# One of seven output products split once more into seven, over two couples of row tiles

## Chip, cores and metric

The kernel runs on one core of a Trainium2 chip. The metric is the device time of one execution in microseconds. Three runs of the kernel before gave a median of 860.69 us (860.5 to 860.8).

## The reference

`x` is [2048, 640]. The kernel computes attention over the last 512 cached keys of 32 heads of width 192, projects the result back to 640 columns, and gates it with a feed-forward block:

```python
xn = _layernorm(x)
q  = (xn @ wq)                                   # 32 heads of 192
p  = softmax(q @ k[-512:].T * 192 ** -0.5)
s  = concat_heads(p @ v[-512:]) @ wo             # [2048, 6144] @ [6144, 640]
g  = _silu((silu(xn @ w_gate) * (xn @ w_up)) @ w_down)
return x + s * g
```

The change concerns only `s`, that is the product with `wo`, and how it is computed for 12 of the 16 row tiles.

## The kernel before, in words

First the layer norm and the feed-forward block are computed; `g` goes to a DRAM buffer, `g_d`. Then come 32 phases of attention, whose order is written out by hand in tables of tokens. The attention output is transposed by DMA and written to DRAM, `o_d`, as 16 row tiles of 128 rows with 48 chunks of the contraction of 128 each. The output part multiplies it with `wo`.

In the output part, a **couple** is a pair of row tiles (`ROW_PAIRS`, eight couples, numbered 0 to 7). For a couple the product is a 2 x 2 block product: the left matrix has quarters A11, A12 (first row tile, the two halves of the contraction) and A21, A22 (second row tile); `wo` has quarters B11 to B22, split by contraction half and column half. A quarter on the left is 24 chunks of 128 x 128; on the right 24 chunks of 128 x 320. The eight block products are replaced by seven (M1 to M7, in the order M1, M7, M2, M5, M6, M4, M3) with sums of quarters on both sides (`A_OF`, `B_OF`). `product` (L1201) issues one of them: 24 matmuls of 320 columns into one PSUM bank, each with its own weight load. M2 accumulates in the bank of M1, M4 in that of M7, M3 in that of M5.

- The left sums (`a_sum`, L1193, VectorE, 128 x 3072) take M7 = A11 - A21, M5 = A21 + A22, M6 = M5 - A11, M3 = A12 - M6. They go in turn to two places in `q_all` and to one tile `a_s`, three sums ahead of the product that uses them.
- The right sums (`b_sum`, L1165) are made once, during the end of attention and the first two couples.
- ScalarE copies the banks of M1 and M7 to SBUF (`u` and `v`). VectorE adds the products up there (`total`, L1238) and applies the gate and `x` (`finish`, L1222 and L1223, two operations for a quarter of the output).
- The left quarters lie in four tiles `a_q` for couples of even number and four for odd. `load_a` (L1178, 768 KB) brings couple n+2 into the tiles of couple n: A11 and A21 are issued after M6 of couple n, A12 and A22 after its M4. `load_xg` and `store` bring `x` and `g` in and the result out. All of these stand in order in SyncE's queue (SP).
- Products of couples 0 and 1 alternate; couples 2 to 7 run one after another (`ORDER`).
- In the very last couple, M5 and M3 go as two halves of 160 columns each into two banks, so that the first half can be finished earlier.

Eight PSUM banks serve the output part (`bank`, pool `psum_out`), handed out by the framework as earlier tiles are no longer used.

Of the kernel before, what the change touches and what calls it, by code (L numbers as in the profile page):

```python
# [10 lines left out]
ALU = mybir.AluOpType  # L11
# [4 lines left out]
def kernel(  # L16
# [13 lines left out]
    nc = tc.nc  # L30
    P = nc.NUM_PARTITIONS
# [8 lines left out]
    W = min(4096, max(256, Sk // 4))  # L40
# [10 lines left out]
    KH = NPAIR * PD // P // 2  # L51
    HC = D // 2
# [4 lines left out]
    h16 = dt.float16  # L57
# [23 lines left out]
    def mm_tile(which=None):  # L81
# [11 lines left out]
    q_all = qpool.tile([P, 16, 512], bf, name="q_all")  # L93
# [5 lines left out]
    A11, A12, A21, A22 = range(4)  # L99
    M1, M7, M2, M5, M6, M4, M3 = PRODUCTS = range(10, 17)  # L100
    A_OF = {
        M1: (A11,), M2: (A12,), M4: (A22,),
        M7: (A11, A21, ALU.subtract), M5: (A21, A22, ALU.add), M6: (M5, A11, ALU.subtract),
        M3: (A12, M6, ALU.subtract),
    }
# [152 lines left out]
    a_q, b_w = {}, {}  # L258
# [882 lines left out]
    def load_b(m, pool=None, eng=nc.scalar, c0=0, c1=KH):  # L1141
        if m in b_w:
            pass
        elif pool is None:
            b_w[m] = xc[:, 0:3, :, :].rearrange("p s c n -> p (s c n)").rearrange("p (c d) -> p c d", d=HC)
        else:
            b_w[m] = b_tile(m, pool)[:, :, :]
        if eng is None:
            return
        to = b_w[m][:, c0:c1, :]  # L1150
        eng.dma_start(out=to.bitcast(bf) if m in B_SUMS else to, in_=wo_quarter(m, c0, c1))
# [28 lines left out]
    late, a_s, xg = [], {}, {}  # L1180

    def a_sum(n, m):
        x, y, op = A_OF[m]
        k = len(a_s) % 3
        if k == 2:
            a_s[n, m] = late[0].tile([P, KH, P], h16, name="a_s", tag="a_s")
        else:
            a_s[n, m] = q_all[:, 8 * k : 8 * k + 6, :].bitcast(h16).rearrange("p a (c n) -> p (a c) n", n=P)

        def part(q):  # L1190
            return a_s[n, q] if q in A_OF and (n, q) in a_s and len(A_OF[q]) == 3 else a_q[n, q][:]

        nc.vector.tensor_tensor(a_s[n, m][:] if k == 2 else a_s[n, m], part(x), part(y), op)  # L1193
# [12 lines left out]
    def load_xg(n):  # L1206
        for side, r in enumerate(ROW_PAIRS[n]):
            tag, bufs = ("khat", 2) if n % 2 == 0 else (("K_p", "KT")[side], 1)
            t = xg[n, side] = kpool.tile([P, 2, D], bf, name="xg", tag=tag, bufs=bufs)
            nc.sync.dma_start(out=t[:, 0, :], in_=x2[r * P : (r + 1) * P, :])  # L1210
            nc.sync.dma_start(out=t[:, 1, :], in_=g_d[r, :, :])
# [17 lines left out]
    V = nc.vector  # L1229

    ORDER = [(n, m) for ms in ((M1, M7), (M2,), (M5,), (M6,), (M4,), (M3,)) for n in range(2) for m in ms][1:]
    ORDER += [(n, m) for n in range(2, len(ROW_PAIRS)) for m in PRODUCTS]
    A_SUMS = [nm for nm in ORDER if len(A_OF[nm[1]]) == 3]

    acc = {}
# [4 lines left out]
    def bank(n, name):  # L1240
        acc[n, name] = late[1].tile([P, 512], f32, name="acc")[:, 0:HC]
        return acc[n, name]
# [16 lines left out]
    def run(n, m):  # L1259

        ahead = n + 2 < len(ROW_PAIRS)
        u, v, c = (f_tile(n, k) for k in range(3))
        if m == M1:
            ps = bank(n, "M1+M2")
            product(n, M1, ps)
            nc.scalar.copy(u, ps)  # L1266
        elif m == M7:
            ps = bank(n, "M7+M4")
            product(n, M7, ps)
            nc.scalar.copy(v, ps)  # L1270
        elif m == M2:
            ps = acc[n, "M1+M2"] if n else bank(n, "M2")
            product(n, M2, ps, first=n == 0)
            if n == 0:
                total(f_tile(n, 3), ps, u)
            finish(n, 0, 0, ps if n else f_tile(n, 3), in_psum=n > 0)
            if (n, M3) == ORDER[-1]:
                store(n, 0, slice(0, HC))
        elif m == M5:
            pss = [bank(n, "M5+M3"), bank(n, "M5+M3'")] if (n, M3) == ORDER[-1] else [bank(n, "M5+M3")]  # L1280
            product(n, M5, pss)
            w = HC // len(pss)
            for k, ps in enumerate(pss):
                total(v[:, k * w : (k + 1) * w], ps[:, 0:w], v[:, k * w : (k + 1) * w])
        elif m == M6:
            ps = bank(n, "M6")
            product(n, M6, ps)
            total(u, ps, u)
            total(v, u, v)
            finish(n, 1, 1, v)  # L1290
            for q in (A11, A21) if ahead else ():
                load_a(n + 2, q)
        elif m == M4:
            ps = acc[n, "M7+M4"]
            product(n, M4, ps, first=False)
            total(c, ps, u)
            finish(n, 1, 0, c)
            for q in (A12, A22) if ahead else ():
                load_a(n + 2, q)
            store(n, 1)  # L1300
        else:
            ps, t, last_cols = acc[n, "M5+M3"], xg[n, 0], slice(HC, D)
            if (n, m) == ORDER[-1]:
                total(u, u, t[:, 1, last_cols], ALU.mult)
                total(u, u, t[:, 0, last_cols])
                pss = [ps, acc[n, "M5+M3'"]]
                product(n, M3, pss, first=False)
                w = HC // len(pss)
                for k, ps in enumerate(pss):
                    part, cols = slice(k * w, (k + 1) * w), slice(HC + k * w, HC + (k + 1) * w)  # L1310
                    total(c[:, part], ps[:, 0:w], t[:, 1, cols], ALU.mult)
                    total(t[:, 0, cols], c[:, part], u[:, part])
                    store(n, 0, cols, (nc.sync, nc.scalar)[k])
            else:
                product(n, M3, ps, first=False)
                total(u, ps, u)
                finish(n, 0, 1, u)
                store(n, 0)
            if ahead:
                load_xg(n + 2)  # L1320
        if (n, m) in A_SUMS:
            k = A_SUMS.index((n, m)) + 3
            if 3 < k < len(A_SUMS):
                a_sum(*A_SUMS[k])

    FIRST = (
# [40 lines left out]

    AHEAD = task_tables()
    groups, units = {}, {}
    wide = None  # L1370

    def group_of(s, kind):

# [28 lines left out]
             "wc": combine_wq, "wp": lambda pr: combine_wq(pr, 2), "j": join_wq}[what[:-1]](pr, *n)  # L1402

    def token(s, x):
        nonlocal wide

        cp, ph = divmod(s, 4)
        if x[0].isdigit():
            context_unit(s, *x.split("."))
        elif x[0] == "s" and x[1].isdigit():  # L1410
            scores(first_step(s) + int(x[1]) // KC, int(x[1]) % KC)
        elif x[:2] == "sp":
            spill(first_step(s) + int(x[2]))
        elif x[:2] in ("DG", "JG"):
            q_diag(JOINT if x[0] == "J" else 1 if ph < 2 else 0, *x[2:])
        elif x[0] in "RJ":
            group_of(s, x[0])[x[1]](*x[2:])
        elif x[:2] in ("TT", "QQ"):
            k, j = (int(x[2]), 2) if x[0] == "T" else divmod(int(x[2]), 2)
            q_rows(first_step(s + 1) + k, j, int(x[3]))  # L1420
        elif x == "ah":
            if s in AHEAD:
                what, *args = AHEAD[s]
                what(*args)
        elif x[:2] == "vl":
            pr = 2 * cp + (1 if x[2] == "O" else 2 if s else 0)
            if pr < NPAIR:
                load_v(pr)
        elif x == "free":
            actx.close()  # L1430
            wide = ctx.enter_context(tc.tile_pool(name="out_b", bufs=1, reuse_waits="tile"))
            O_last = wide.tile([P, 2, 4, 2, Dh], bf, name="O_last")
            O_late.extend(O_last[:, k, :, :, :] for k in range(2))
        elif x[:3] == "lM5":
            n = int(x[3])
            load_b(M5, None, nc.sync, n * KH // 4, (n + 1) * KH // 4)
        elif x[0] == "l":
            load_a("AB".index(x[1]), int(x[2]))
        elif x[:2] == "xg":
            load_xg(int(x[2]))  # L1440
        elif x[:2] == "bm":
            b_sum(M7, int(x[2]))
        elif x[0] == "o":
            first_product(int(x[1]))
        elif x == "as0":
            a_sum(*A_SUMS[0])
        else:
            what, n = (x[:-1], (int(x[-1]),)) if x[-1].isdigit() else (x, ())
            of_pair(s, what, n)
# [26 lines left out]
    for k, (n, m) in enumerate(ORDER):  # L1476
        run(n, m)
        for step in sums.get((n, m), ()):
            b_sum(*step)
        if (n, m) == (1, M1):  # L1480
            a_sum(*A_SUMS[3])
        if k < 4:
            load_b(M3, late[0], nc.sync, k * KH // 4, (k + 1) * KH // 4)


# [28 lines left out]
```

## Time and profile before

| | |
|---|---|
| median of three runs | 860.69 us (860.5 to 860.8) |
| the profiled execution, its time | 860.93 us |
| its span in the profile | 859.0 us |
| TensorE busy, in the span | 854.2 us, 99% |
| VectorE busy | 601.7 us, 70% |
| ScalarE busy | 456.4 us, 53% |
| granted TensorE clock | 1.0 |
| output part: couples 2 to 7 begin with M1 at | 718.56 us |
| last product begins at | 852.28 us |

The span runs from the first to the last instruction of the profiled execution; what lies around it is the difference to its time. PE is TensorE's matmuls, PEld its weight loads, DVE VectorE, ACT ScalarE, SP SyncE's DMA queue. A matmul's own duration overlaps that of the next, so what one costs is seen from the distance between starts.

### The profile page before, as it was taken

How to read it: one execution, taken by the hardware profiler on the slowest of the kernel's cores; microseconds unless marked ns; L12 is line 12 of the kernel's file. 1: busy time of each engine (PE TensorE's matmuls, PEld its weight loads, DVE VectorE, ACT ScalarE, POOL GpSimd, SP SyncE). 2: the span in 40 equal slices, each digit the busy share in tenths (PEclk: the TensorE clock that was granted, in tenths of full speed). 3: DMA queues.
4: the chain of work that ended last, by engine and by line, in shares of the span. 5: the costliest groups of instructions: out<-in, count | busy, mean ns of one | idle time of the engine just before them, and what ended most of it. 6: DMA issues, size and time to landing. Idle time of an engine off the chain costs nothing.

```text
span 859.0 us, 23271 instructions
## 1 busy us (share of the span) xinstructions
PE 854.2 (99%) x9839; PEld 571.5 (67%) x9839; DVE 601.7 (70%) x1059; ACT 456.4 (53%) x611; POOL 165.6 (19%) x247
## 2 busy tenths in 40 slices
PE   9999999999999999999999999999999999999998
PEld 6456446577667667667667667667677777777776
DVE  6687987877758758757757767767657796555564
ACT  4574675657667666676676676676766500000000
POOL 0010000103324324324323323323412000000000
PEclk9999999999999999999999999999999999999999
DMA  9879314556787799998999996899699998745400
GB/s 294 180 139 214 77 35 108 133 94 157 179 176 127 184 206 178 192 216 176 200 210 191 198 174 147 185 186 197 161 158 195 284 294 293 253 153 188 168 27 16
DMA packets 271496, 149.14 MB, mean 174 GB/s; under 512 B 174112, under 2 KB 267296, under 8 KB 271392
## 3 DMA queue, kind: packets, MB, share of 16 engines
q1 hardware_dynamic: 270608, 147.01, 75.3%
q8 instruction: 77, 1.26, 0.7%
q10 hardware_dynamic: 784, 0.65, 0.3%
q14 instruction: 27, 0.22, 0.1%
HBM read 80.51 MB, written 30.41 MB: 129 GB/s over the span
## 4 chain that ended last, share of the span: by engine, by line
PE 99%; DMA 1%; SPq 0%; DVE 0%; issue 0%
PE acc L1201 21%; PE sc L1047 19%; PE mm L1085 13%; PE mm L990 13%; PE sc L990 7%; PE sc L1085 6%; PE sc L394 6%; PE mm L479 3%; PE mm L637 3%; PE sc L637 2%; PE sc L479 2%; PE mm L978 1%; PE sc L690 1%; DMA wg_sb<-in_B_w_gate_dram 1%; PE gu L394 0%; PE mm L1251 0%
## 5 line engine op out<-in xcount | busy, mean ns | idle before, releaser
L1051 ACT ACTIVATE p_t<-sc 128x1024 bf16<-128x1024 f32 x256 | 256.9, 1025 | 93.9 <-PE sc L1047 93.2
L1047 PE MATMUL sc<-q_all,khat 64*128 64x512 bf16 x1536 | 204.5, 376 | 0.0
L1085 PEld LDWEIGHTS <-p_t 64*128 64x128 bf16 x4096 | 180.2, 94 | 35.2 <-POOL turn_t L1063 0.3
L1085 PE MATMUL mm<-V_p,p_t 64*128 64x193 bf16 x2784 | 146.9, 243 | 0.0
L990 PEld LDWEIGHTS <-w_all 64*128 64x128 f16 (+1 forms) x1540 | 87.3, 94 | 72.8
L990 PE MATMUL mm<-xc,w_all 64*128 64x512 f16 x950 | 119.4, 376 | 0.0
L1047 PEld LDWEIGHTS <-khat 64*128 64x128 bf16 x1536 | 83.2, 94 | 50.8 <-issue 2.4
L1032 POOL TENSOR_TENSOR m_f<-m_f 128x1024 f32<-128x1024 f32 x44 | 104.8, 2381 | 41.9 <-DVE q_all L1028 40.6
L1028 DVE TENSOR_TENSOR q_all<-mm,m_f 128x1024 bf16<-128x1024 f32 x44 | 53.8, 1223 | 70.3 <-ACT m_f L1025 70.3
L1201 PE MATMUL acc<-b_w,a_q 128*128 128x320 bf16 (+1 forms) x552 | 78.4, 299 | 0.0
L1107 DVE TENSOR_TENSOR O_b<-mm,r 128x384 bf16<-128x384 f32 x142 | 73.8, 553 | 2.9
L1266 ACT COPY xc<-acc 128x320 f32<-128x320 f32 x7 | 3.0, 426 | 133.9 <-PE acc L1201 98.5
L1063 POOL MEMSET turn_t<- 128x1 f32 x128 | 12.8, 100 | 317.3 <-PE mm L1085 224.7
L1038 DVE TENSOR_TENSOR q_all<-mm,m_f 128x1024 bf16<-128x1024 f32 x44 | 53.8, 1222 | 22.6 <-POOL m_f L1032 22.2
L1085 PE MATMUL sc<-V_p,p_t 64*128 64x193 bf16 x1312 | 68.0, 243 | 0.0
L1201 PEld LDWEIGHTS <-a_q 128*128 128x128 bf16 x552 | 54.0, 98 | 21.0
L1201 PEld LDWEIGHTS <-q_all 128*128 128x128 f16 x552 | 52.6, 98 | 19.2 <-issue 0.2
L1201 PE MATMUL acc<-b_w,q_all 128*128 128x320 f16 (+2 forms) x432 | 58.1, 292 | 0.0
L1025 ACT COPY m_f<-sc 128x1024 f32<-128x1024 f32 x37 | 37.4, 1012 | 29.5 <-PE sc L990 29.4
L990 PE MATMUL sc<-xnT,w_all 64*128 64x512 bf16 x370 | 46.6, 376 | 0.0
L1103 DVE RECIPROCAL r<-mm 128x4 f32<-128x4 f32 x87 | 15.7, 181 | 36.1 <-PE mm L1085 34.3
L173 DVE TENSOR_TENSOR w_all<-wq_rows 64x640 f16<-64x640 bf16 x90 | 38.7, 482 | 0.5
(176 smaller groups left out, 1019.0 us busy)
## 6 DMA issues: line engine op xcount, KB each, us to landing
o_d<-OT_b SPq DMA_DIRECT2D x64, 384.0 KB, 3.8
a_q<-o_d SPq DMA_DIRECT2D x32, 768.0 KB, 6.8
wq_rows<-in_A_wq_dram SPq DMA_DIRECT2D x16, 480.0 KB, 5.1
b_w<-in_A_wo_dram SPq DMA_DIRECT2D x16, 480.0 KB, 6.3
wq_rows<-in_A_wq_dram SPq DMA_DIRECT2D x30, 240.0 KB, 5.9
K_p<-in_A_k_cache_dram SPq DMA_DIRECT2D x32, 192.0 KB, 3.7
V_p<-in_A_v_cache_dram SPq DMA_DIRECT2D x32, 192.0 KB, 3.9
xc<-xnT SPq DMA_DIRECT2D x10, 320.0 KB, 4.7
```

What stands on the lines that cost most here:

```text
L394: nc.tensor.matmul(out, w_sb[:, c, f * P : (f + 1) * P], xnT[:, c, qc], start=(c == 0), stop=(c == NC - 1),)
L479: nc.tensor.matmul(ps, left[:, c, :], D_OF[m][:, c, :], start=(first and c == 0), stop=(c == KD - 1), skip_group_check=True,)
L637: nc.tensor.matmul(ps[:, h, :], left[m][r, c, n * P : (n + 1) * P], RIGHT[m][r, c, :], start=(first and c == 0), stop=(c == NC - 1), skip_ ...
L990: nc.tensor.matmul(ps[:, h, :], ws[h][r, c, :], xs[h][r, c, :], start=(first and c == 0), stop=(c == NC - 1), skip_group_check=True,)
L1028: nc.vector.tensor_tensor(to[:, 1:3, :], st["ps"][:, :, :], m_f[:, 5:3:-1, :], ALU.add)
L1032: nc.gpsimd.tensor_tensor(SIDE, diag, SIDE, ALU.subtract)
L1038: nc.vector.tensor_tensor(to[:, 0:4:3, :], st["ps"][:, :, :], SIDE, ALU.add)
L1047: nc.tensor.matmul(sc[:, h, :], khat[r, j, ks], q_of(i, j)[r, :], start=(j == 0), stop=(j == 2))
L1051: nc.scalar.activation(p_t[:, :, :], sc[:, :, :], ACT.Exp, scale=scale)
L1085: m = nc.tensor.matmul(acc[:, k, h * 256 : h * 256 + Dh + 1], Ps[i][kc][r, h, qt * P : (qt + 1) * P], V_of[i // NB % 2][r, kc, h, 0 : Dh + 1],
L1107: nc.vector.tensor_tensor(O_b[:, k, :, :], a_k[:, :, 0:Dh], r[:, k, :, :].to_broadcast([P, 2, Dh]), ALU.mult,)
L1201: nc.tensor.matmul(ps[:, 0:w], at[:, c, :], b_w[m][:, c, k * w : (k + 1) * w], start=(first and c == 0), stop=(c == KH - 1), skip_group_ch ...
```

## The change

Couples 2 to 7 are run in three pairs of couples (2 with 3, 4 with 5, 6 with 7) by a new function, `run_pair`. M1, M7, M2, M5, M4 and M3 of both couples are issued as before, alternating between the two. M6 of the two couples has the same right-hand matrix, so the two M6 products together are one block product of a left matrix of two row tiles by the right matrix of M6. This is again cut in two along each dimension, and seven inner products of 12 matmuls of 160 columns each take its place. Their left sums (`inner_left`) are of 1536 elements a partition, four for a pair; their right sums (`inner_right`) are of 1920, four in all, made once between M4 of couple 1 and M2 of couple 2. The inner products go to three banks U, V and W; VectorE adds each of them to the running sums in SBUF as soon as it is there, and U and W are accumulated further after that.

The left sums M5, M6 and M3 of these couples are written over A21, A11 and A12 in the `a_q` tiles. M7's goes to the `a_s` tile. Loads for the next pair are issued where the tiles come free in the new order. Nothing changes in the attention part, and couples 0 and 1 keep their products.

```diff
-    ORDER += [(n, m) for n in range(2, len(ROW_PAIRS)) for m in PRODUCTS]
+    LAST_ROWS = len(ROW_PAIRS) - 1
...
-            if (n, M3) == ORDER[-1]:
+            if n == LAST_ROWS:
                 store(n, 0, slice(0, HC))
...
             finish(n, 1, 1, v)
-            for q in (A11, A21) if ahead else ():
+            for q in (A11, A21):
                 load_a(n + 2, q)
         elif m == M4:
...
-            for q in (A12, A22) if ahead else ():
+            for q in (A12, A22) if n < 2 else (A22,) if ahead else ():
                 load_a(n + 2, q)
             store(n, 1)
...
             if ahead:
+                if n > 1:
+                    load_a(n + 2, A12)
                 load_xg(n + 2)
...
+    IN_PLACE = {M5: A21, M6: A11, M3: A12}
+    K2, C2 = KH // 2, HC // 2
+
+    def pair_left(n, m):
+        x, y, op = A_OF[m]
+        if m in IN_PLACE:
+            a_s[n, m] = a_q[n, IN_PLACE[m]][:].bitcast(h16)
+        else:
+            a_s[n, m] = late[0].tile([P, KH, P], h16, name="a_s", tag="a_s")[:]
+        x, y = (a_s[n, q] if q in (M5, M6) else a_q[n, q][:] for q in (x, y))
+        nc.vector.tensor_tensor(a_s[n, m], x, y, op)
...
+    def inner_right():
...
+        steps = [(t1, q12, q11), (t2, q22, t1), (q12, q22, q12), (t4, q21, t2)]
+        return {M1: q11, M2: q21, M5: t1, M6: t2, M7: q12, M3: q22, M4: t4}, [
+            lambda to=to, x=x, y=y: total(to, x, y, ALU.subtract) for to, x, y in steps
+        ]
+
+    def inner_left(n):
+        (l11, l12), (l21, l22) = (halves(a_s[n + k, M6]) for k in range(2))
+        s1, s2 = halves(late[0].tile([P, KH, P], h16, name="a_s", tag="a_s")[:])
+        s3, s4 = halves(a_q[n, A21][:].bitcast(h16))
+        return {M1: l11, M2: l12, M5: s1, M6: s2, M7: s3, M3: s4, M4: l22}, [
...
+                (s1, l21, l22, ALU.add), (s2, s1, l11, ALU.subtract),
+                (s3, l11, l21, ALU.subtract), (s4, l12, s2, ALU.subtract),
...
+    def run_pair(n, right, after):
+        o, ahead = n + 1, n + 3 < len(ROW_PAIRS)
...
+        do(n, M1)
+        do(n, M7)
+        pair_left(o, M7)
+        pair_left(o, M5)
+        do(o, M1)
+        pair_left(n, M6)
+        do(o, M7)
+        pair_left(o, M6)
+        do(n, M2)
+        left, sums = inner_left(n)
+        sums[0]()
+        sums[1]()
+        do(o, M2)
+        pair_left(n, M3)
+        pair_left(o, M3)
+        do(n, M5)
+        sums[2]()
+        sums[3]()
+        do(o, M5)
+        more(o, A21)
+        (un, vn), (uo, vo) = ((f_tile(t, 0), f_tile(t, 1)) for t in (n, o))
+        U, V, W = (bank(n, "M6" + x)[:, 0:C2] for x in "UVW")
+
+        def inner(m, ps, to, k, first=True):
+            for c in range(K2):
+                nc.tensor.matmul(
+                    ps, left[m][:, c, :], right[m][:, c, :],
+                    start=(first and c == 0), stop=(c == K2 - 1), skip_group_check=True,
+                )
+            if to is not None:
+                to = to[:, k * C2 : (k + 1) * C2]
+                total(to, ps, to)
+
+        inner(M1, U, un, 0)
+        inner(M5, W, uo, 1)
+        inner(M2, V, un, 0)
+        more(n, A11)
+        inner(M6, U, un, 1, False)
+        inner(M3, W, un, 1, False)
+        inner(M7, U, uo, 1, False)
+        more(n, A21)
+        total(vn, un, vn)
+        finish(n, 1, 1, vn)
+        do(n, M4)
+        inner(M4, U, uo, 0, False)
+        more(o, A11)
+        total(vo, uo, vo)
+        finish(o, 1, 1, vo)
+        do(o, M4)
+        do(n, M3)
+        if ahead:
+            pair_left(n + 2, M7)
+            pair_left(n + 2, M5)
+        do(o, M3)
...
+        if (n, m) == (1, M4):
+            right, steps = inner_right()
+            steps[0]()
+        elif (n, m) == (0, M3):
+            pair_left(2, M7)
+            pair_left(2, M5)
+    for n in range(2, len(ROW_PAIRS), 2):
+        run_pair(n, right, {(3, M1): steps[1:2], (3, M7): steps[2:3], (2, M2): steps[3:]} if n == 2 else {})
```

`do(t, m)` is `run(t, m)` followed by the right-hand sums that `after` names for that place; `more(t, q)` is `load_a(t + 2, q)` where there is a next pair.

More of the change, by code (lines that the diff above doesn't have):

```diff
@@ L1276, in run @@
             finish(n, 0, 0, ps if n else f_tile(n, 3), in_psum=n > 0)
-            if (n, M3) == ORDER[-1]:
+            if n == LAST_ROWS:
                 store(n, 0, slice(0, HC))
         elif m == M5:
-            pss = [bank(n, "M5+M3"), bank(n, "M5+M3'")] if (n, M3) == ORDER[-1] else [bank(n, "M5+M3")]
+            pss = [bank(n, "M5+M3"), bank(n, "M5+M3'")] if n == LAST_ROWS else [bank(n, "M5+M3")]
             product(n, M5, pss)
@@ L1302, in run @@
             ps, t, last_cols = acc[n, "M5+M3"], xg[n, 0], slice(HC, D)
-            if (n, m) == ORDER[-1]:
+            if n == LAST_ROWS:
                 total(u, u, t[:, 1, last_cols], ALU.mult)
@@ L1324, in run, with halves @@
                 a_sum(*A_SUMS[k])
+    IN_PLACE = {M5: A21, M6: A11, M3: A12}
[8 more added lines that the diff above has]
+        nc.vector.tensor_tensor(a_s[n, m], x, y, op)
+    def halves(t):
+        return t[:, 0:K2, :], t[:, K2:KH, :]
@@ new lines, in inner_right, with piece @@
+    def inner_right():
+        q11, q12, q21, q22 = (
+            b_w[M6][:, k * K2 : (k + 1) * K2, c * C2 : (c + 1) * C2] for k in range(2) for c in range(2)
+        )
+        def piece(t):
+            return t[:, 0 : K2 * C2].rearrange("p (c d) -> p c d", d=C2)
+        t1 = piece(O_last[:, :, :, :, :].rearrange("p a b c d -> p (a b c d)").bitcast(h16))
+        t2, t4 = (
+            piece(q_all[:, 8 * k : 8 * k + 6, :].rearrange("p a n -> p (a n)").bitcast(h16)) for k in range(2)
+        )
+        steps = [(t1, q12, q11), (t2, q22, t1), (q12, q22, q12), (t4, q21, t2)]
+        return {M1: q11, M2: q21, M5: t1, M6: t2, M7: q12, M3: q22, M4: t4}, [
+            lambda to=to, x=x, y=y: total(to, x, y, ALU.subtract) for to, x, y in steps
+        ]
@@ new lines, in inner_left @@
+    def inner_left(n):
[3 more added lines that the diff above has]
+        return {M1: l11, M2: l12, M5: s1, M6: s2, M7: s3, M3: s4, M4: l22}, [
+            lambda to=to, x=x, y=y, op=op: total(to, x, y, op) for to, x, y, op in (
+                (s1, l21, l22, ALU.add), (s2, s1, l11, ALU.subtract),
+                (s3, l11, l21, ALU.subtract), (s4, l12, s2, ALU.subtract),
+            )
+        ]
@@ new lines, in run_pair, with do, more @@
+    def run_pair(n, right, after):
+        o, ahead = n + 1, n + 3 < len(ROW_PAIRS)
+        def do(t, m):
+            run(t, m)
+            for step in after.get((t, m), ()):
+                step()
+        def more(t, q):
+            if ahead:
+                load_a(t + 2, q)
+        do(n, M1)
[25 more added lines that the diff above has]
+                    start=(first and c == 0), stop=(c == K2 - 1), skip_group_check=True,
+                )
+            if to is not None:
[18 more added lines that the diff above has]
+        do(n, M3)
+        if ahead:
+            pair_left(n + 2, M7)
+            pair_left(n + 2, M5)
+        do(o, M3)
@@ L1369 @@
     groups, units = {}, {}
-    wide = None
+    wide = O_last = None
     def group_of(s, kind):
@@ L1404, in token @@
     def token(s, x):
-        nonlocal wide
+        nonlocal wide, O_last
         cp, ph = divmod(s, 4)
```

## The prediction

> **What bounds the kernel now.** I read the page from the top: busy time per engine, the slices, the chain that ended last.
>
> ```profile
> PE 854.2 (99%) x9839; PEld 571.5 (67%) x9839; DVE 601.7 (70%) x1059; ACT 456.4 (53%) x611; POOL 165.6 (19%) x247
> PEclk9999999999999999999999999999999999999999
> PE 99%; DMA 1%; SPq 0%; DVE 0%; issue 0%
> ```
>
> The chain that ended last is TensorE for 99% of the span, and the granted clock is full throughout. So the time is the sum of the matmuls' pitches, and only two things can move it: fewer TensorE nanoseconds, or a wait that does not exist today. I therefore opened the timeline of TensorE over the output part, the stretch that the change touches. The columns are start, duration and instructions; a duration contains 0.16 us of overlap with the next group, so a product's price is the distance from one start to the next.
>
> ```profile
> 718.56 3.42 PE L1201 MATMUL acc<-b_w,a_q 128*128 128x320 bf16 x24
> ...
> 839.18 3.42 PE L1201 MATMUL acc<-b_w,a_q 128*128 128x320 bf16 x24
> 842.44 3.48 PE L1201 MATMUL acc<-xc,a_s 128*128 128x160 f16 x48
> 845.76 3.42 PE L1201 MATMUL acc<-b_w,q_all 128*128 128x320 f16 x24
> 849.02 3.42 PE L1201 MATMUL acc<-b_w,a_q 128*128 128x320 f16 x24
> 852.28 3.48 PE L1201 MATMUL acc<-b_w,q_all 128*128 128x160 bf16 x48
> ```
>
> 718.56 is M1 of couple 2. From there to 842.44 lie 38 products without one gap: 123.88/38 = 3.26 us each, 135.8 ns a matmul of 320 columns. The last couple's M5 is already cut in two halves of 160 columns, each with its own weight load: 48 matmuls in 845.76 - 842.44 = 3.32 us, 69.2 ns each. That row is exactly the shape the change introduces. The weight loads in that same stretch:
>
> ```profile
> 842.31 3.42 PEld L1201 LDWEIGHTS <-a_s 128*128 128x128 f16 x48
> ```
>
> 48 loads, one for each narrow matmul, and they keep the pace.
>
> **What the change takes off TensorE.** M6 of two couples is now 2 x 24 wide matmuls, 2 x 3.26 = 6.52 us. Afterwards it is seven inner products of 12 matmuls of 160 columns: 84 x 69.2 ns = 5.81 us, 0.83 us each. Saved: 0.71 us for two couples, and there are three such pairs (2+3, 4+5, 6+7): 3 x 0.71 = 2.13 us. The other 36 products of these couples, the first two couples and the attention part keep their matmuls. Order within a pair changes (products of the two couples alternate), at no TensorE price by itself.
>
> A rule of the Trainium skill speaks against this. Its page "TensorE: Matmul & The Clock Gate", section "Back-to-back issue gap", says that in a stream of weight load and matmul pairs both set the spacing, about 81 ns for 128 columns. Since 160 columns cannot be cheaper, the inner products would cost at least 84 x 81 ns = 6.80 us, an estimate, and the change would lose 0.28 us a pair. The trace disagrees here, with 69.2 ns at 160 columns and a load each time, and I go by the trace.
>
> **What it adds to VectorE.** Durations from the output part's groups:
>
> ```profile
> L1193 DVE TENSOR_TENSOR q_all<-a_q 128x3072 f16<-128x3072 bf16 x11 | 19.2, 1749 | 0.1
> L1165 DVE TENSOR_TENSOR b_w<-b_w 128x1920 f16<-128x1920 bf16 x4 | 4.6, 1151 | 0.0
> L1238 DVE TENSOR_TENSOR xc<-acc,xc 128x160 f32<-128x160 f32 x2 | 0.7, 325 | 2.0 <-PE acc L1201 2.0
> ```
>
> A pair now has eight left sums (8 x 1.75 = 14.0 us) and 26 operations of 320 columns (0.49 each, 12.7): 26.7 us in 14 x 3.26 = 45.64 us. The change keeps the eight sums, adds four inner left sums of 1536 elements (0.95 us each, on the line through 1920 and 3072 elements: 3.8), adds seven totals of 160 columns (0.33: 2.3) and drops the two totals of M6 (1.0): 31.8 us in 44.93 us, 71%. The first pair also has three of the four inner right sums (1920 elements, 1.15 each; the fourth lies in couples 0 and 1): 35.3 us, 79%. VectorE does not become the bound, so what counts is whether an individual operation is late. I laid the instructions of a middle pair in program order with these durations, VectorE starting 0.20 us after a product's nominal end (845.96 against 845.76 for the total after M5). Zero is the start of the pair's M1:
>
> - Second couple's M7 sum: it goes into the one a_s buffer, so it waits for the first M7 (6.52), runs 6.72 to 8.47, needed at 9.78.
> - M5 and M6 sums in place: done at 13.7. M5 is needed at 19.56 and 22.82.
> - First two inner left sums: 17.5 to 19.4, behind the finish of M2; needed at 26.91 and 28.57.
> - Both M3 sums to 24.3, total of the first M5, last two inner left sums to 26.66; needed at 29.40 and 30.23.
> - Inner products: M1 at 26.08, M5 26.91, M2 27.74, M6 28.57, M3 29.40, M7 30.23. M6 accumulates onto bank U after the total of M1 has read it (27.48, margin 1.09). M7 accumulates onto U after the total of M6: that runs 29.60 to 29.93, margin 0.30. It is the tightest point of the whole pair.
> - In the first pair VectorE runs later by the right sums, the total of M1 ends at 28.31, margin 0.26.
>
> So each added wait costs nothing if VectorE's end reaches TensorE in under 0.26 to 0.30 us. Rows that bear on it:
>
> ```profile
> 0.91 0.27 DVE L267 MEMSET q_all<- 128x256 uint32 x1
> 1.24 4.66 PE L323 MATMUL gu<-q_all 128*128 128x512 bf16 x15 [1.24 <-DVE q_all L267]
> ...
> 595.58 0.10 POOL L1063 MEMSET turn_t<- 128x1 f32 x1 [2.53 <-PE mm L1085]
> ...
> 595.92 0.60 PE L1085 MATMUL mm<-V_p,p_t 64*128 64x193 bf16 x10
> ```
>
> The first matmul starts 0.06 us after the VectorE write that releases it. In the attention part a matmul follows 0.24 us after the GpSimd memset that it waits for, and TensorE had no gap there. No row shows a VectorE release tighter than that under a running stream, so the wait's price is bounded by 0 from 0.06 us, and by 0.1 us a pair if the way takes 0.4. I take 0, being nearest to the first row; what queues behind a late M7 is M4 and all of TensorE, so any excess is paid in full. A gain is excluded, since TensorE has no idle time to give back.
>
> **Banks.** The pair holds seven of the eight PSUM banks at once (eight in the last pair). Today M5 starts at 751.16 while VectorE reads the bank of M2 from 751.36 on, so a new bank is not the one just read; I cost this at nothing. If it were, M5 of the second of a pair would wait for one read of about 0.7 us.
>
> **Loads and SP's queue.** Because M6, M5 and M3's left sums now lie in the a_q tiles, the loads for the next pair start later: second A21 after M5, first A11 and A21 within the inner products, second A11 after the inner M4, A22 after M4, A12 only after M3, each behind the stores ahead of it on SP's queue. By the same layout the issues come from -18.8 us (before the next pair) to +4.05 us. The latest, A12 of the second couple, is needed by its M2 at +16.30, 12.2 us later; A12 of the first has 14.0 us; A22 of the second about 15. Cover is thus the four M1 and M7 products ahead of the M2s.
>
> ```profile
> a_q<-o_d SPq DMA_DIRECT2D x24, 768.0 KB, 6.5
> 700.00:720.00 20.00, 20.00 (x149) 14.42 (x148) 16.77 (x25) 0.00 (x0) 0.00 (x0) 1.00 1.04 386
> ```
>
> A load lands after 6.5 us (median of the output part; 12.2 at the longest, with six in a row). The bunch is 7.4 MB up to A12 of the second couple; the last column of the window's row shows 386 GB/s sustained. I cost it at nothing.
>
> **Tail.** The last couple ends as before, with the same five VectorE operations ahead of the last halves. One 160 KB store is newly close to the end, issued about 1.5 us before the last matmul ends, and lands after 2.4 us; the last 40 KB store leaves 0.76 us after that end. Cost 0 to 0.2 us; I take 0.
>
> **Sum.** The profiled execution took 860.93 us, span 859.0, with 1.93 around it: span 856.9, time 858.8. The median of the runs is 0.24 lower, so 858.6.
>
> **Rivals.**
> - *A bubble at bank U* (chance 0.17). If VectorE's end takes x us to reach TensorE, x over 0.30 costs x - 0.30 in each pair, plus x - 0.26 once. At x = 0.6: 0.9 + 0.34 = 1.24 us, 859.8. At 0.4, 0.44, 859.0. For it: TensorE now really follows VectorE within a microsecond, which the output part nowhere did before. Against it: the 0.06 and 0.24 us above. A bank wait at M5 (3 x 0.7, 860.7) is the worse variant of the same kind.
> - *Late loads* (0.07), the one on the other side. Place: M2 of the second couple, twice (before pairs 4+5 and 6+7). The bunch must pass in the 33 us between its first transfer and 16.3 us, 225 GB/s. Below 213 GB/s the wait exceeds 1.93 us each time, and the kernel is slower than before by over 0.2%. At half of 386, 193 GB/s, A12 lands at about 21.9, 5.6 us late twice: 858.6 + 11.2 = 869.8. Against it: 386 GB/s in the row shown.
> - *Narrow matmuls at the pace of weight loads* (0.03). One load lasts 98 ns in the groups; if loads did not overlap, 84 x 98 ns = 8.23 us, 1.71 more than now, 865.8. By the page named above the bound alone gives 858.6 + 3 x 0.99 = 861.5, an estimate. Against it: the 48 loads in 3.32 us.
>
> **Numbers.** My forecast, no new wait of weight, has 0.70; 0.03 stays for what I do not see, on the slow side. About 0.2% (1.72 us) is what a measurement of this kernel can tell from no change; the forecast clears it by 0.41 us only, so a bubble above x = 0.39 already makes it "same". Faster: 0.70 and a small part of the bubble case, 0.72. Same: 0.16. Slower: 0.12, late loads, load pace and the unseen. The range reaches from 858.2 (runs scatter by 0.15) to 861.0, which takes in the bubbles and the bank wait and leaves the slow cases out.
>
> **What would show it.** Right: three stretches of 72 and 12 narrow matmuls at 69.2 ns, M4 of the first couple between them, pair starts 44.9 us apart, TensorE without idle time, VectorE near 71% there. Wrong: idle time before the third or last of the first six inner products released by VectorE's total (bubble); idle before M2 released by a_q's DMA (late loads); a pitch of 81 to 98 ns in the narrow matmuls (load pace).

## The result, and the profile after

The changed kernel takes 858.48 us (median of 10 runs, 858.15 to 859.56) against 860.86 us for the kernel before in the same rounds: ratio 0.9974, 95% interval 0.9964 to 0.9984. That is 2.38 us less, and the whole interval lies below 1. The forecast was 858.6 us in a range of 858.2 to 861.0. The profiled execution took 858.21 us, its span 856.4.

Busy time and the chain that ended last, from the page of the changed kernel:

```profile
PE 851.6 (99%) x9947; PEld 574.0 (67%) x9947; DVE 619.9 (72%) x1090; ACT 456.2 (53%) x611; POOL 164.1 (19%) x247
PE 99%; DVE 0%; DMA 0%; issue 0%; ACT 0%; DVEq 0%
```

TensorE is still the whole chain, with 2.6 us less work in 108 more matmuls; VectorE has 18.2 us more. The timeline of TensorE in the middle pair of couples, which begins at 763.04; L1412 is the inner product's matmul:

```profile
753.26 13.20 PE L1201 MATMUL acc<-b_w,a_q 128*128 128x320 f16 x96
...
789.12 0.99 PE L1412 MATMUL acc<-b_w,a_q 128*128 128x160 f16 x12
789.95 0.99 PE L1412 MATMUL acc<-O_last,a_s 128*128 128x160 f16 x12
790.78 0.99 PE L1412 MATMUL acc<-b_w,a_q 128*128 128x160 f16 x12
791.61 0.99 PE L1412 MATMUL acc<-q_all,a_s 128*128 128x160 f16 x12
792.44 1.82 PE L1412 MATMUL acc<-b_w,a_q 128*128 128x160 f16 x24
794.10 3.42 PE L1201 MATMUL acc<-b_w,a_q 128*128 128x320 f16 x24
797.36 0.99 PE L1412 MATMUL acc<-q_all,a_q 128*128 128x160 f16 x12
798.19 13.20 PE L1201 MATMUL acc<-b_w,a_q 128*128 128x320 f16 x96
```

The first row holds the last three wide products of the pair before, 3.26 us each, and then the M1 with which this pair begins, at 753.26 + 9.78 = 763.04. Every inner product stands 0.83 us after the one ahead of it: M1, M5, M2, M6, and M3 with M7 in one row of 24, which takes 1.66 us to the M4 at 794.10. The first inner product stands 26.08 us after the pair's start, as laid out. The last row is built like the first, so the next pair's M1 starts at 807.97, 44.93 us after this one. No row shows idle time. What TensorE waited for in the whole execution, over 0.2 us, is a single line, and it stands at the kernel's beginning:

```profile
PE gu L323 <- DVE q_all L267: 1.2, 1, 1.2
```

### The profile page after: what moved, and what is told of

Its sections match the earlier page's. It is cut to its first block, busy times and chain, and to the rows that moved or that the text cites. A ratio compares the mean times of both kernels' runs of the same rounds, so it can differ in the third digit from the quotient of the medians.

```text
span 856.4 us, 23528 instructions
## 1 busy us (share of the span) xinstructions
PE 851.6 (99%) x9947; PEld 574.0 (67%) x9947; DVE 619.9 (72%) x1090; ACT 456.2 (53%) x611; POOL 164.1 (19%) x247
## 4 chain that ended last, share of the span: by engine, by line
PE 99%; DVE 0%; DMA 0%; issue 0%; ACT 0%; DVEq 0%
PE sc L1047 19%; PE acc L1201 19%; PE mm L1085 14%; PE mm L990 13%; PE sc L990 7%; PE sc L1085 6%; PE sc L394 6%; PE mm L479 3%; PE mm L637 3%; PE sc L637 2%; PE sc L479 2%; PE acc L1412 2%; PE mm L978 1%; PE sc L690 1%; PE gu L394 1%; PE mm L1251 0%
## 5 line engine op out<-in xcount | busy, mean ns | idle before, releaser
L1201 PEld LDWEIGHTS <-a_q 128*128 128x128 bf16 (+1 forms) x888 | 84.1, 98 | 29.8
L1201 PE MATMUL acc<-b_w,a_q 128*128 128x320 bf16 (+2 forms) x720 | 97.2, 295 | 0.0
L1238 DVE TENSOR_TENSOR xc<-acc,xc 128x320 f32<-128x320 f32 (+1 forms) x48 | 19.5, 410 | 23.3 <-PE acc L1201 15.0
L1113 ACT ACTIVATE O_b<-mm,r 128x192 bf16<-128x192 f32 x56 | 20.5, 417 | 22.1 <-DVE r L1103 17.8
```

The costliest lines, as they stand in the source:

```text
L1201: nc.tensor.matmul(ps[:, 0:w], at[:, c, :], b_w[m][:, c, k * w : (k + 1) * w], start=(first and c == 0), stop=(c == KH - 1), skip_group_ch ...
```

## The experiments

Theory A says that only TensorE's matmul pitch moved, three times 0.71 us, and that the waits and loads that the change adds are covered. The rivals are those of the prediction, and one more that the result suggested: that the order or the loads gave something themselves, since 2.38 is more than 2.13.

**The changed kernel again.** No edit.

> The changed kernel once more, as the reference for the others on the same chip. Theory A (only TensorE's matmul pitch moved, 0.71 us in each of three pairs): 2.1 us under the kernel before in the same rounds, and the pairs 44.93 us apart. Rival B (more than the matmuls moved, since the first median lay 2.4 us lower and the profiled span 2.6 us): 2.4 to 2.6 us under it, with a step of 0.3 to 0.5 us that comes back between the same two places of the program.

858.51 us (8 runs) against 861.03: ratio 0.9973 (0.9963 to 0.9984). So the gain repeats, 2.5 us, and is not separable from 2.13 by the interval, which spans about 1.4 to 3.2 us. The medians alone leave the 0.4 us above 2.13 open. The traces settle where it lies: from couple 2's M1 to the end of the span are 140.44 us in the kernel before (718.56 to 859.0), 138.29 in the changed kernel (718.11 to 856.4) and 138.33 in this run (718.37 to 856.7). The stretch that the change touches is thus 2.1 us shorter both times, as theory A has it. What comes on top in these executions lies ahead of it, 0.45 us the first time and 0.19 the second, and is not the step of 0.3 to 0.5 us that rival B asked for.

**Order only.** M6 back in one piece:

```diff
-        U, V, W = (bank(n, "M6" + x)[:, 0:C2] for x in "UVW")
-        inner(M1, U, un, 0)
-        ...                      # the other inner products and their sums
+        for t, u in ((n, un), (o, uo)):
+            ps = bank(t, "M6")
+            product(t, M6, ps)
+            total(u, ps, u)
+            ...                  # loads, total and finish of the first couple
```

> Pairs, alternating order, sums in place and the later loads stay; only M6 of each couple goes back to one product of 24 matmuls of 320 columns, and the inner sums are gone. Theory A: all of the gain goes, pairs 45.64 us apart, 2.1 us over the changed kernel, level with the kernel before. Rival B, the order or the loads bring something themselves: it stays 0.3 us or more under the kernel before.

860.84 us against 861.03, ratio 0.9999 (0.9991 to 1.0008), 2.33 us over the changed kernel. From TensorE's timeline of this run:

```profile
718.84 3.42 PE L1201 MATMUL acc<-b_w,a_q 128*128 128x320 bf16 x24
744.92 22.98 PE L1201 MATMUL acc<-b_w,a_q 128*128 128x320 f16 x168
```

The row of 168 contains six products of this pair and the next pair's M1, which starts 6 x 3.26 = 19.56 us after 744.92, at 764.48: 45.64 us after 718.84. The medians alone, 0.19 us apart with an interval of some 0.7 us to either side, would not exclude a step of 0.3 us; the trace does, with 140.46 us from couple 2's M1 to the end of the span (718.84 to 859.3) against 140.44 before. Alternating the couples, summing in place and loading later bring nothing and cost nothing there. The whole gain of that stretch is the split, and rival B falls.

**Two dependent inner products side by side.** The order that the change chose puts M3 between M6 and M7:

```diff
-        inner(M6, U, un, 1, False)
         inner(M3, W, un, 1, False)
+        inner(M6, U, un, 1, False)
         inner(M7, U, uo, 1, False)
```

> The inner products in the order M1, M5, M2, M3, M6, M7, so that M7, which accumulates onto the bank that M6 has filled, follows M6 directly. The matmuls are the same. Theory A with waits paid in full: TensorE idles before M7 for 0.20 us to VectorE's start, 0.33 us of its total and x back, 0.6 us in each pair with x = 0.06, and x can be read; 1.8 us over the changed kernel, so nearly nothing is left of the gain. Rival: the wait is hidden by the weight loads pulled ahead or by the pipeline, idle under 0.2 us a pair, and the order that was chosen does not matter.

860.35 us, ratio 0.9991 (0.9982 to 0.9999): 1.84 us over the changed kernel, with 1.8 expected. The timeline at the place, TensorE's M6, VectorE's total of it, TensorE's M7:

```profile
793.41 0.99 PE L1412 MATMUL acc<-q_all,a_s 128*128 128x160 f16 x12
794.45 0.33 DVE L1238 TENSOR_TENSOR xc<-acc,xc 128x160 f32<-128x160 f32 x1 [0.51 <-PE acc L1412]
794.82 0.99 PE L1412 MATMUL acc<-b_w,a_q 128*128 128x160 f16 x12 [0.42 <-DVE xc L1238]
```

M6 ends nominally at 794.24, VectorE starts 0.21 us later, works 0.33 us, and TensorE goes on 0.04 us after VectorE's end. M7 starts 0.58 us late, the same in the three pairs: 1.74 us. The 0.42 in brackets is the idle time after the modelled end of the last matmul and understates it; the distance from start to start is what is paid. This run also measures x of the prediction, the way from VectorE's end to TensorE: 0.04 us.

**Narrower matmuls.** On the order-only kernel, M6 of each couple in four parts of 80 columns and then in eight of 40, a weight load for each:

```diff
-            product(t, M6, ps)
+            product(t, M6, [ps[:, 80 * k : 80 * (k + 1)] for k in range(4)])
```

> As e1, with M6 of each couple in four parts of 80 columns, a weight load for each matmul: 192 matmuls of 80 columns a pair. If the pitch stays a line through 135.8 ns at 320 and 69.2 ns at 160 columns, 35.9 ns each: 6.89 us a pair against 6.52, 1.1 us over e1 in all. Rival C, weight loads set the pace below some width: a pitch of 50 ns or more, at 55 ns 10.6 us a pair, 12 us over e1; the pitch then tells the width under which splitting a product further brings nothing.

> As the run with 80 columns, with M6 of each couple in eight parts of 40: 384 matmuls of 40 columns a pair, a weight load each. The line through 320, 160 and 80 columns (135.8, 69.2 and 35.8 ns) gives 19.2 ns at 40: 7.37 us a pair against 6.52 in one piece, 2.6 us over the run in wide pieces (order only) in all. Rival C again, a weight load must take some time of its own that 80 columns still cover: the pitch stays between 19.2 and 35.8 ns; at 30 ns 11.5 us a pair, 15 us over in all. The pitch found is the floor under which a narrower cut saves nothing.

80 columns: 861.68 us, 0.84 over the order-only run, 1.1 expected. 40 columns: 872.85 us, 11.7 over the kernel before in the same rounds (861.13), with which the order-only run was level; 2.6 were expected. The rows of TensorE's timeline, first the 80-column run from M6 to the next pair's M7, then the same stretch of the middle pair with 40 columns:

```profile
744.30 23.34 PE L1201 MATMUL acc<-b_w,a_q 128*128 128x80 f16 x312
767.48 3.42 PE L1201 MATMUL acc<-b_w,a_s 128*128 128x320 f16 x24
```

```profile
795.90 26.11 PE L1201 MATMUL acc<-b_w,a_q 128*128 128x40 f16 x504
821.86 3.42 PE L1201 MATMUL acc<-b_w,a_s 128*128 128x320 f16 x24
```

Each stretch holds five wide products, 16.30 us. What is left is 23.18 - 16.30 = 6.88 us for 192 matmuls, 35.8 ns each, and 25.96 - 16.30 = 9.66 us for 384, 25.2 ns each. 35.8 is on the line through 320 and 160 columns, with every weight load hidden; 25.2 is not (19.2). So at 80 columns rival C, with 50 ns or more, falls. At 40 its "30 ns" was too much, but its kind of floor is there, well under the 160 columns of the change. Whether the weight load or the matmul itself sets this floor, no run here separates. In the first pair of the 40-column run TensorE also stood still for 1.64 us, for nothing that the profile names, and the granted clock was 0.66 on average from 752 to 757 us; that pair cost 5.7 us more than M6 in wide pieces instead of 3.1. Why it stood still stays open.

**More traffic in the bunch of loads.** Copies of 768 KB from DRAM to DRAM behind the loads of couples 4 to 7, four or eight for each transition (`COPIED` names two of the four quarters or all of them):

```diff
         eng.dma_start(out=a_q[n, q][:, cs, :], in_=src)
+        if n > 3 and q in COPIED:
+            eng.dma_start(out=spare[n, :, q * KH : (q + 1) * KH, :], in_=src)
```

> The changed kernel with four copies of 768 KB from one DRAM buffer to another for each of the two transitions between pairs, each right behind the load of A11 or A21 on SP's queue; nothing reads the copies. The bunch up to A12 of the second couple grows from 7.4 to 10.5 MB. Theory A (loads have room: they must pass in 33 us, that is 10.5 MB at 318 GB/s, and 386 GB/s was seen): A12 lands about 6 us before its M2, no wait, level with the changed kernel. Rival late loads, with a rate in the bunch of 280 GB/s or less: a wait at M2 of the second couple, 4 us or more twice.

> The same with eight copies for each transition, one behind every load: 13.7 MB up to A12 of the second couple. Theory A: at 386 GB/s that takes 35.5 us, A12 of the second couple lands 2.6 us after its M2 could start; TensorE then waits in front of M2, about 1 us for the first couple and 1.6 us for the second, twice: 5 us over the changed kernel. So the rival late loads is a real one, with its point at somewhat under twice the traffic. If there is no wait, the point lies further off than worked out.

Four copies: 858.60 us (the kernel before took 860.93 in these rounds and in those of the run after it), level with the changed kernel, no wait of TensorE in the output part. Eight copies: 859.92 us (858.85 to 860.72), ratio 0.9985 (0.9976 to 0.9994), 1.4 us over the changed kernel, with 5 expected. Two stretches of five microseconds of the eight-copy run (the last column is GB/s, the one ahead of it the DMA engines' busy share), and the matmul that waited:

```profile
760.00:765.00 5.00, 5.00 (x39) 3.60 (x38) 4.90 (x6) 0.00 (x0) 0.00 (x0) 1.00 1.02 412
775.00:780.00 5.00, 4.70 (x36) 3.19 (x34) 2.11 (x2) 0.43 (x1) 0.00 (x0) 1.00 1.03 405
```

```profile
779.81 3.43 PE L1205 MATMUL acc<-b_w,a_q 128*128 128x320 bf16 x24 [0.30 <-DMA a_q<-o_d]
```

The place is one of those named, M2 of the second couple; the rate was 412 GB/s and not 386, so 13.7 MB take 33.3 us, and A12 was due some 0.4 us late instead of 2.6. From start to start this M2 is 0.46 us late: the M2 before it stands at 776.09, and 3.26 us later is 779.35. The first couple's M2, for which 1 us was expected, did not wait, and the M2s of the last pair lost only 0.06 us. This execution, 858.85 us, is the fastest of the run's eleven; where the others lost their further microsecond is not in a trace. So late loads are a real way to lose part of the gain, but their point lies at nearly twice the traffic that the change has, and that they cost the whole 1.4 us is not shown.

**More of VectorE.** The first inner left sum three times, same result:

```diff
         sums[0]()
+        sums[0]()
+        sums[0]()
         sums[1]()
```

> The first inner left sum is computed three times instead of once, 1.9 us more of VectorE in each pair ahead of the inner products, same result. VectorE then has 75% in a middle pair. Theory A (an instruction's lateness counts, not the share): VectorE's queue reaches the total of the inner M1 late, TensorE waits before the inner M6 that accumulates onto the same bank: 1.7 us in the first pair, 0.6 us in each other, 2.9 us in all, which is more than the change has gained. Rival, idle VectorE time hides it: no wait, level with the changed kernel.

859.40 us, ratio 0.9979 (0.9970 to 0.9988): 0.9 us over the changed kernel. Expected were 2.9. The inner M6 of the first pair, from TensorE's timeline:

```profile
747.59 0.99 PE L1414 MATMUL acc<-q_all,a_s 128*128 128x160 f16 x12 [0.78 <-DVE xc L1238]
```

It stands 29.52 us after this pair's start at 718.07 where 28.57 is due: 0.95 us late, released by VectorE's total. The other two pairs show no wait, where 0.6 us each was expected. So the mechanism is right and idle share does not hide it, but my layout of VectorE's queue was late by about 0.8 us (below).

## Why the prediction was right, point by point

**TensorE's term, 3 x 0.71 us: right, and it is the whole gain.** Pairs 44.93 us apart in the changed kernel and 45.64 in the order-only one, both as worked out from the rows of the kernel before. The row that decided it was the last couple's M5 in two halves: it already showed the new shape at 69.2 ns.

**The rule of the Trainium skill on narrow matmuls: not borne out.** "TensorE: Matmul & The Clock Gate", section "Back-to-back issue gap", gives about 81 ns at 128 columns for a stream with weight loads. Here 80 columns take 35.8 ns with a load each. The kernel before runs the rule's own shape as well, which the prediction leaves out: in its feed-forward part (L394), groups of five matmuls of 128 columns, with five loads, start at 13.94 and 14.22 us, 56 ns a matmul. The same page, in "Wait — 56ns, not 53.3ns?", names a floor of about 25 ns from start to start however narrow the matmul is; with that the trace of the narrowest cut agrees, 25.2 ns at 40 columns.

**Bank U, cost 0: right.** In the changed kernel this is VectorE's total of M6 in the middle pair:

```profile
792.64 0.32 DVE L1238 TENSOR_TENSOR xc<-acc,xc 128x160 f32<-128x160 f32 x1 [0.51 <-PE acc L1412]
```

It ends at 792.96, 0.04 us to TensorE makes 793.00, and M7 is due at 793.27, 0.83 us after M3: margin 0.27 after the way back, as against the 0.24 (0.30 less x = 0.06) that the prediction left. The adjacent order shows what it would have cost: 0.58 us a pair.

**VectorE's layout: harmless, but mis-sized.** I let each instruction start when the one before it had ended. In the trace, one that does not read the result just written starts 0.08 to 0.09 us earlier: in the middle pair

```profile
787.07 0.49 DVE L1238 TENSOR_TENSOR xc<-acc,xc 128x320 f32<-128x320 f32 x1
787.47 0.95 DVE L1238 TENSOR_TENSOR a_q<-a_q 128x1536 f16<-128x1536 f16 x1
788.33 0.95 DVE L1238 TENSOR_TENSOR a_q<-a_q,a_s 128x1536 f16<-128x1536 f16 x1
```

0.40 and 0.86 us lie between starts, for durations of 0.49 and 0.95. Over the dozen instructions of the first pair's full queue that is most of a microsecond. In that pair, which begins at 718.11, the total of the inner M1 is the second of these two:

```profile
744.87 0.72 DVE L1238 TENSOR_TENSOR xc<-acc,xc 128x320 f32<-128x320 f32 x2
```

It ended 27.5 us after the pair's start, not 28.31, so its margin was about 1.09 us, not 0.26; the error lay on the safe side. The experiment with two more sums was off in its size by the same step. VectorE's share was 69% in the middle pair (30.90 of 44.93 us) where 71% was worked out, and 75% in the first (33.83 of 44.93 us) where it was 79%.

**Loads, cost 0: right.** The latest, A12 of the second couple, was issued at 767.44, 4.40 us after the pair's start (4.05 worked out), and loads landed after 4.3 to 7.1 us around there; 16.3 was the deadline. Over five microseconds the bunch ran at up to 346 GB/s ahead of the middle pair and 372 ahead of the last; with eight copies behind it, DMA gave 412. The added wait that this term put at nothing did not come.

**Banks and tail, cost 0: right.** No M5 waits; from the start of VectorE's last instruction to the end of the span are 2.84 us before and 2.82 after.

**The 0.25 us above the sum.** The median fell by 2.38 instead of 2.13, the profiled span by 2.6. In the span, 2.15 lie in the stretch that the change touches, and the rest ahead of it: couple 2's M1 starts at 718.56 before and at 718.11 after. That place moves from one execution to another; in the ten traces it lies between 718.07 and 718.84. In some it follows the first load of `w_gate`, with which the chain then begins: its length and the start of the output part are 5.06 us and 718.22 (80 columns), 5.38 and 718.51 (adjacent), 5.54 and 718.56 (before), 5.81 and 718.84 (order only). The changed kernel's own chain begins with a load of rows of `x` instead, so that load alone does not explain its 718.11. The scatter is as large as the excess. That the excess of the medians has the same cause is likely, not shown.

## What to carry to other kernels

Before costing a new instruction shape from a rule, look for the shape in the trace; here one couple already ran it, and that row settled the sign. Where TensorE is the whole chain, a small cut in matmuls is paid out in full only if each new accumulation has a neighbour that does not depend on it: here, putting two dependent inner products side by side lost 1.8 of the 2.1 us. Test a margin by adding to it, a sum or a copy at a time, because a busy share of 70% says nothing on which instruction is late.

## What the runs showed of the hardware

- With a weight load each, matmuls took 135.8, 69.2 and 35.8 ns at 320, 160 and 80 columns, and 25.2 ns at 40. Down to 80 columns a further cut costs about 2.5 ns for each matmul added (2 x 69.2 - 135.8 = 2.6, 2 x 35.8 - 69.2 = 2.4); from 80 to 40 it costs 14.6 ns.
- TensorE resumed 0.04 us after the VectorE instruction that it waited for (run with two dependent inner products side by side); the way in the other direction was 0.20 to 0.21 us from the nominal end of the product.
- A VectorE instruction that did not read the result just written started 0.08 to 0.09 us before the recorded end of the one ahead of it (first and middle pair of the changed kernel).
- DMA loads and copies together held 405 to 416 GB/s from 750 to 780 us of the run with eight copies, with the engines' share at 1.0.
